# An attention and MLP kernel whose first block runs all scores first, with weights' sums of squares two to four tiles ahead

## Chip, cores and metric

The kernel runs on one core of a Trainium2 chip. The metric is the device time of one execution in microseconds (us), the median over runs.

## The reference

The program is a causal attention with decay, followed by two feed-forward layers. Batch 4, 8 heads, 576 positions, head size 64, model width 512. The part that this document is about is the attention and the first layer:

```python
scores = scale * np.matmul(q, k.transpose(0, 1, 3, 2))
decay = cum[:, :, :, None] - cum[:, :, None, :]        # cum = cumsum(log f)
scores = np.where(causal, -1000000000.0, scores + decay)
attn = np.exp(scores - np.max(scores, axis=-1, keepdims=True))
attn = attn / (np.sum(attn, axis=-1, keepdims=True) + 1e-09)
attn_out = np.matmul(attn, v)
...
xn = (x - mu) / np.sqrt(var + 1e-06) * g_ln            # mu, var over the 512 columns of x
x = x + np.maximum(xn @ w_ch1, 0.0) @ w_ch2            # w_ch1 512x2048, w_ch2 2048x512
...
return (gated @ w_out)                                 # second layer, untouched by the change
```

The weights arrive as 64-bit floats, so the kernel reads each as two 32-bit words.

## The kernel before, in words

The 4 x 576 rows are cut into eight blocks of 256 rows (`BLOCKS`) and a rest, and each block goes through attention, a normalisation and the first layer. Blocks 0 and 1 hold the first 128 positions of two batch entries each; their attention is `attention32`, in f32. It takes the heads in four pairs `p` (p0 to p3), and a pair has four 128x128 squares (two batch entries, two heads):

- scores (L356): the contraction has 66 rows, 64 of the head and two that bring the decay. VectorE (DVE) adds the mask and takes the minimum (L359), ScalarE (ACT) takes the exponential and its sum (L361), then the sums get their 1e-9 (L364) and DVE their reciprocal (L365).
- transposes (L373): a matmul of `e` with `diag`, a diagonal of the reciprocals that DVE writes (L369), which transposes and normalises in one. ACT copies the result out as `PT` (L374).
- P.V (L381): `PT` times the values `vr`, per batch entry once with 128 columns of `vr` and once with the first 64 overwriting the upper half; ACT copies it out as `xT` (L382).

Before these come the loads and the decay rows (`decays`, L146): ScalarE takes the logarithm of `f`, VectorE scans it, and a small tile `decay` goes by two DMAs into the last two rows of `qk` (L343). `WARM` = 54 matmuls of a tile of ones run on TensorE in the meantime (L1064).

The first layer of block 0 (group 0 of `mlp`, L654) is in f32: for each of 16 weight tiles, `ph` (L708) is the product with `w_ch1`, ACT's relu gives `hh` (L715), and `acc` (L693) adds the product with `w_ch2`, two tiles later (`AHEAD`). In the same stretch the kernel narrows every raw weight tile from 64 to 32 bits (`narrow`, L518: two ACT instructions L531 and L532 that write `wt` and `low`, three DVE instructions L533 to L535), adds up the squares of the weights on TensorE (`squares`, L561, into `gram`), and takes from them a scale (`scales`, L575). With the scale it splits each tile into two f16 halves (`make16`, L593: ACT L598, DVE L601) that groups 1 to 7 multiply with. Three raw tiles fit (`RAWB`), and a raw tile's load can start when the third one before it has been narrowed.

The order on each engine comes from a scheduler, which takes the instructions in the order of `events` (L1119 to L1145) and from ordering edges (`after`, L123). `PACE` and `LOWAT` place the ACT work of the first tiles behind marks; `SUMS` says which `ph` waits for the scale; `WSC`, `MAKE` and `VN` are the due times of `scales`, `make16` and `vnorm` (L228, the sums of squares of the values).

Of the kernel before, what the change touches and what calls it, by code (L numbers as in the profile page):

```python
# [30 lines left out]
BUFS0 = dict(vr=1, qk=1, e=3, diag=2, PT=2, st=4)  # L31
# [8 lines left out]
WARM = 54  # L40
# [46 lines left out]
class Kernel:  # L87
# [58 lines left out]
    def decays(self, wk):  # L146


        nc = self.nc
        n = B * H  # L150

        ft = wk.tile([n, S], F32, name="ft")
        for c, queue in ((0, nc.sync), (2 * H, nc.scalar)):
            queue.dma_start(out=ft[c : c + 2 * H], in_=self.f[c : c + 2 * H].rearrange("(n h) s -> h n s", n=2))
        nc.scalar.preload_act_table_set("natural_log_exp_and_others")
        decay = self.decay = self.at.tile([n, 2, 2 * P], F32, name="decay")
        dec1 = wk.tile([n, 2, 3 * P], F32, name="dec1")
# [3 lines left out]
        for t, r, w in ((decay, 1, P), (dec1, 1, P), (f32(dec), 2, S)):  # L161
            nc.gpsimd.memset(t[:, :r, w:], 1.0)
            nc.gpsimd.memset(t[:, r:, :w], 1.0)
        lg = wk.tile([n, S], F32, name="lg")
        cum = wk.tile([n, S], F32, name="cum")

        for cs in (slice(0, P), slice(P, S)):
            nc.vector.tensor_scalar(out=ft[:, cs], in0=ft[:, cs], scalar1=1e-4, scalar2=1.0, op0=ALU.max, op1=ALU.min)
            nc.scalar.activation(lg[:, cs], ft[:, cs], AF.Ln)
            if cs.start:  # L170
                nc.vector.tensor_tensor(out=lg[:, P : P + 1], in0=lg[:, P : P + 1], in1=cum[:, P - 1 : P], op=ALU.add)
            nc.vector.tensor_tensor_scan(out=cum[:, cs], data0=one[:, cs], data1=lg[:, cs], initial=0.0, op0=ALU.mult, op1=ALU.add)
# [8 lines left out]
        nc.scalar.activation(dec[:, 2, S:], f32(h), AF.Copy, scale=-1.0)  # L181
        nc.scalar.activation(dec[:, 3, S:], f32(l), AF.Copy, scale=-1.0)
        nc.scalar.dma_start(out=self.gT, in_=self.moe_g_ln)
        self.gscale(wk)
# [3 lines left out]
    def gscale(self, wk):  # L188

        nc = self.nc  # L190
        g = wk.tile([P, DM], F32, name="gall")
# [3 lines left out]
        nc.scalar.dma_start(out=g, in_=self.moe_g_ln.rearrange("p k -> (p k)").partition_broadcast(P))  # L195
        nc.vector.tensor_reduce(out=m, in_=g, axis=mybir.AxisListType.X, op=ALU.max, apply_absolute_value=True)
# [126 lines left out]

    def attention32(self, b, xT):
# [9 lines left out]
        tags = ("s2", "s2", "av") if b else ("acc", "ph", "av")  # L334
        qka = at.tile([66, NP, 2, 2, 2 * P], F32, tag="qk", name="qk", bufs=bufs["qk"])
# [14 lines left out]
        for p in range(NP):  # L350
            qk, vr = qka[:, p], vra[:, :, p * P : (p + 1) * P]
            ps, e, diag = bank(tags[0]), four("e"), four("diag")
            st = at.tile([P, 2, 4], F32, tag="st", name="st", bufs=bufs["st"])
            four_ = [(n, u, 2 * n + u) for n in range(2) for u in range(2)]
            for n, u, c in four_:
                mm(ps[:, n, u], lhsT=qk[:, u, n, :P], rhs=qk[:, u, n, P:], start=True, stop=True, skip_group_check=True)  # L356
# [9 lines left out]
            yield  # L366

            ps, pt = bank(tags[1]), four("PT")
# [3 lines left out]
            for n, u, c in four_:  # L372
                mm(ps[:, n, u], lhsT=e[:, n, u], rhs=diag[:, n, u], start=True, stop=True, skip_group_check=True)  # L373
# [4 lines left out]
            for n in range(2):  # L378
# [3 lines left out]
            nc.scalar.activation(xT[:, p].rearrange("p (n w) -> p n w", n=2), pav[:, 0], AF.Copy)  # L382
# [135 lines left out]
    def narrow(self, raw, tmp, low=None):  # L518
# [10 lines left out]
        else:  # L529
# [3 lines left out]
            nc.vector.tensor_scalar(out=a, in0=a, scalar1=F64_LO * 2.0**16, scalar2=F64_HI * 2.0**16, op0=ALU.max, op1=ALU.min)  # L533
            nc.vector.scalar_tensor_tensor(out=low, in0=hi, scalar=0x80000000, in1=low, op0=ALU.bitwise_and, op1=ALU.bitwise_or)
            nc.vector.scalar_tensor_tensor(out=b, in0=b, scalar=3, in1=low, op0=ALU.logical_shift_left, op1=ALU.bitwise_or)  # L535
# [3 lines left out]
    def load_raw(self, j):  # L539
# [6 lines left out]
        nc.sync.dma_start(out=raw[:, DM:], in_=self.moe_w_ch2[cs, :])  # L546

    def load_w(self, j):
# [5 lines left out]
        first = self.narrow(raw, w, self.st.tile([P, 2 * DM], U32, tag="low", name="low", bufs=2))  # L554
# [3 lines left out]
        if j < len(LOWAT):  # L558
            self.after(self.low, self.done[LOWAT[j]])

    def squares(self, j):  # L561
# [52 lines left out]
    def norm(self, x, s, y, whole, end, c):  # L614
# [9 lines left out]
        for t in range(NK):  # L624
            nc.vector.tensor_tensor(out=c[:, t, :], in0=x[:, t, :], in1=pm, op=ALU.subtract)
# [28 lines left out]
    def mlp(self, g, states, y):  # L654
# [386 lines left out]
    def run(self):  # L1041
# [20 lines left out]
        warm, ones = self.bank("s2"), self.ones.bitcast(BF16)  # L1062
        for i in range(WARM):
            self.nc.tensor.matmul(warm[:, : 2 * P], lhsT=ones[:, :P], rhs=ones, start=True, stop=True)  # L1064
# [17 lines left out]
        def prep(n):  # L1082
# [25 lines left out]
            g = self.norm(xT, s, y, g > 0, n >= last - 1, xc)  # L1108
            while True:
# [16 lines left out]
        events += [(MAKE + 0.02 * j if j < SOON else G1 + 0.5 * (j - SOON + 0.5) / (NF + 1), -1, NF + 2 + j) for j in range(NF)]  # L1126
        events += [(WSC, -1, NF + 1)] + [(VN + 0.05 * i, -1, NF) for i in range(B + 2)]
        events += [(at, -2, j) for j, at in enumerate(RAWAT)]
# [152 lines left out]
```

## Time and profile before

| | us |
|---|---|
| median of three runs | 790.7 |
| lowest and highest | 788.97, 794.69 |
| the profiled execution | 788.37 |
| its span (first to last instruction) | 786.7 |
| TensorE busy in the span | 763.1 |

The profiled execution lies 2.3 us below the median, and its span covers all but 1.7 us of it. The profile names engines PE (TensorE matmuls), PEld (its weight loads), DVE (VectorE), ACT (ScalarE), POOL (GpSimd) and SP (SyncE, which issues DMAs). L356 is line 356 of the kernel. An f32 matmul is recorded as two matmuls, so "x8" behind one stands for four in the code.

### The profile page before, as it was taken

What the parts mean: (1) busy time and instruction counts of PE and PEld (TensorE: products, weight loads), DVE (VectorE), ACT (ScalarE), POOL (GpSimd) and SP (SyncE); (2) the same over time, 40 slices, a digit from 0 to 9 for tenths busy, and PEclk for the clock granted to TensorE, in tenths of its full rate; (3) what the DMA queues carried; (4) which work ended last, traced back from release to release, by engine and by line L of the source; (5) the groups of instructions that cost most, each with busy time, mean ns of one, the idle gap of its engine ahead of it and who ended that gap; (6) DMA issues with size and microseconds to landing.
All of it is one profiled execution on the core that took longest, in us unless ns stands there. A gap on an engine that the chain in (4) does not pass through costs nothing.

```text
span 786.7 us, 16302 instructions
## 1 busy us (share of the span) xinstructions
PE 763.1 (97%) x5978; PEld 581.1 (74%) x5978; DVE 549.5 (70%) x1490; ACT 521.0 (66%) x1315; POOL 59.8 (8%) x89
## 2 busy tenths in 40 slices
PE   8799999999999999999999999999999999999998
PEld 7588887887877877778888888544447668668676
DVE  5699589849389889979858955688425672654634
ACT  5787489849388889878858854485417643656543
POOL 3100011011011001100201100100021000000000
PEclk8999999999999999999999999999999999999999
DMA  8888576366678998997995964831034320000101
GB/s 252 215 308 307 183 221 93 56 153 119 152 201 160 196 242 151 197 204 156 195 184 117 130 97 145 208 125 54 1 64 73 112 69 1 33 29 9 54 1 61
DMA packets 164227, 104.72 MB, mean 133 GB/s; under 512 B 106178, under 2 KB 151362, under 8 KB 164148
## 3 DMA queue, kind: packets, MB, share of 16 engines
q1 hardware_dynamic: 157848, 96.63, 50.5%
q0 software_dynamic: 5296, 5.28, 5.5%
q10 hardware_dynamic: 1004, 1.78, 0.8%
q8 instruction: 47, 0.77, 0.4%
q14 instruction: 32, 0.26, 0.1%
HBM read 64.37 MB, written 15.11 MB: 101 GB/s over the span
## 4 chain that ended last, share of the span: by engine, by line
PE 69%; DVE 13%; ACT 7%; DMA 6%; issue 3%; SPq 1%; POOL 1%; DVEq 0%; ACTq 0%; POOLq 0%
PE ph L708 16%; PE acc L693 14%; PE pb L649 8%; PE pb L650 8%; PE pb L648 8%; PE s L296 3%; PE av L460 3%; DMA vr<-in_v_dram 2%; DVE P L317 1%; PE s L693 1%; PE av L381 1%; DMA PT<-P 1%; PE gram L569 1%; DVE hl L719 1%; DVE wt L601 1%
## 5 line engine op out<-in xcount | busy, mean ns | idle before, releaser
L693 PE MATMUL acc<-hh,wt 128*128 128x256 f16 (+2 forms) x960 | 196.9, 295 | 1.1 <-DVE t L736 0.5
L708 PE MATMUL ph<-xh,wt 128*128 128x256 f16 (+1 forms) x896 | 187.8, 289 | 5.6 <-DVE hl L719 5.0
L708 PEld LDWEIGHTS <-wt 128*128 128x128 f16 x1344 | 127.3, 98 | 52.0 <-issue 13.6
L693 PEld LDWEIGHTS <-wt 128*128 128x128 f16 x1344 | 128.7, 98 | 43.8 <-issue 5.3
L708 PE MATMUL ph<-xl,wt 128*128 128x256 f16 (+1 forms) x448 | 129.6, 289 | 0.0
L693 PE MATMUL acc<-hl,wt 128*128 128x256 f16 (+1 forms) x416 | 115.3, 281 | 0.0
L715 ACT ACTIVATE hh<-ph 128x256 f16<-128x256 f32 (+2 forms) x128 | 51.0, 399 | 58.5 <-PE ph L708 58.3
L719 DVE SCALAR_TENSOR_TENSOR hl<-ph,hh 128x256 f16<-128x256 f32 (+1 forms) x112 | 50.7, 455 | 39.7 <-ACT hh L715 39.3
L261 ACT ACTIVATE P<-sd,st 128x512 f16<-128x512 f32 (+1 forms) x128 | 70.6, 587 | 10.9 <-DVE st L307 9.5
L317 DVE SCALAR_TENSOR_TENSOR P<-sd,st,P 128x384 f16<-128x384 f32 (+1 forms) x96 | 58.7, 634 | 9.3 <-ACT P L261 8.8
L304 ACT ACTIVATE sd<-sd,st 128x384 f32<-128x384 f32 (+2 forms) x80 | 54.6, 682 | 15.1 <-DVE st L300 14.9
L296 PE MATMUL s<-x 68*128 68x384 f32 (+7 forms) x256 | 63.3, 360 | 0.1
L300 DVE CUSTOM_DVE_ANT_0 sd<-s,mask 128x384 f32<-128x384 f32 (+2 forms) x80 | 45.9, 580 | 4.7 <-PE s L296 3.7
L740 POOL DMA_DIRECT2D x_d<-t x36 | 32.4, 1089 | 185.3 <-DVE t L736 148.9
L261 ACT ACTIVATE x<-qk 64x320 fp32r<-64x320 f32 (+1 forms) x64 | 41.4, 698 | 0.9 <-DMA qk<-in_qk_dram 0.9
L1016 DVE SCALAR_TENSOR_TENSOR u<-pb,wsc,u 128x288 f32<-128x288 f32 x32 | 16.0, 515 | 34.5 <-PE pb L1015 34.5
L296 PEld LDWEIGHTS s<-x 68*128 68x128 f32 (+3 forms) x256 | 36.9, 177 | 2.7 <-issue 1.0
L648 PE MATMUL pb<-x2h,wil 128*128 128x288 f16 (+2 forms) x144 | 37.8, 273 | 0.0
L650 PE MATMUL pb<-x2h,wih 128*128 128x288 f16 (+2 forms) x144 | 37.7, 273 | 0.0
L649 PE MATMUL pb<-x2l,wih 128*128 128x288 f16 (+2 forms) x144 | 37.7, 273 | 0.0
L648 PE MATMUL pb<-wsh,vl 128*128 128x288 f16 x128 | 36.6, 286 | 0.1
L650 PE MATMUL pb<-wsh,vh 128*128 128x288 f16 x128 | 36.6, 286 | 0.0
(281 smaller groups left out, 1597.7 us busy)
## 6 DMA issues: line engine op xcount, KB each, us to landing
raw<-in_moe_w_ch_dram SPq DMA_DIRECT2D x32, 512.0 KB
qk<-in_qk_dram SPq DMA_DIRECT2D x32, 448.0 KB
vraw<-in_v_dram SPq DMA_DIRECT2D x5, 1024.0 KB
vr<-in_v_dram SPq DMA_DIRECT2D x16, 320.0 KB
x_d<-xT SPq DMA_DIRECT2D x9, 512.0 KB
x_d<-t POOLq DMA_DIRECT2D x36, 128.0 KB, 4.4
out_dram<-o SPq DMA_DIRECT2D x32, 144.0 KB
raw<-in_moe_w_in_dram SPq DMA_DIRECT2D x8, 512.0 KB
```

Of the source, the lines that this page charges most:

```text
L261: self.nc.scalar.activation(out, in_, AF.Copy, scale=scale)
L296: nc.tensor.matmul(ps[: R * u + R, : c1 - c0], lhsT=x[:, lo - q0 - R * u : hi - q0], rhs=y[:, c0:c1], start=g == 0, stop=g == len(heads[u] ...
L300: nc.vector.tensor_tensor_reduce(out=sd[:M, c0:c1], in0=ps[:M, : c1 - c0], in1=mask, scale=-0.125, scalar=3e38 if n == 0 else st[:M, n - 1 ...
L304: nc.scalar.activation(sd[:M, :N], sd[:M, :N], AF.Exp, bias=st[:M, n : n + 1], scale=-1.0, accum_out=st[:M, 2:3])
L317: low = nc.vector.scalar_tensor_tensor(out=dl, in0=src, scalar=rs, in1=dh, op0=ALU.mult, op1=ALU.subtract)
L648: first = mm(out, lhsT=al, rhs=bh, start=start, stop=False, **kw)
L649: mm(out, lhsT=ah, rhs=bl, start=False, stop=False, **kw)
L650: mm(out, lhsT=ah, rhs=bh, start=False, stop=stop, **kw)
L693: ins = nc.tensor.matmul(acc[m], lhsT=a, rhs=b, start=bank not in clear, stop=last and e == len(terms) - 1, skip_group_check=True)
L708: ins = nc.tensor.matmul(ph, lhsT=a, rhs=b, start=k == e == 0, stop=k == NK - 1 and e == len(terms) - 1)
L715: relu = nc.scalar.activation(hh, ph, AF.Relu)
L719: nc.vector.scalar_tensor_tensor(out=hl, in0=ph, scalar=0.0, in1=hh, op0=ALU.max, op1=ALU.subtract)
```

## The change

The core of the diff (lines left out are "..."):

```diff
-BUFS0 = dict(vr=1, qk=1, e=3, diag=2, PT=2, st=4)
+BUFS0 = dict(vr=1, qk=1, e=4, diag=2, PT=2, st=4)
...
-WARM = 54
+WARM, FILLS = 52, (4, 12, 6)
...
-PACE = (1, "split", "split", "split", "split")
-LOWAT = (1, 2, 3)
-SUMS = 13
+PACE = (1, "x3", "split", "split", "split")
+LOWAT = (1, "x3", "split")
+SUMS = 14
+REST = 0.1
+SQ = (1, 3, 4, 5, 6, 8, 9, 10, 12, 13, 14, 16)
...
-WSC, MAKE, VN = 0.63, 0.64, 0.7
+WSC, MAKE, VN = 0.76, 0.765, 0.82
...
+    def fill(self, n, behind=None):
+        ones = self.ones.bitcast(BF16)
+        for i in range(n):
+            ins = self.nc.tensor.matmul(self.warm[:, : 2 * P], lhsT=ones[:, :P], rhs=ones, start=True, stop=True)
...
@@ attention32
+        if not b:
+            self.vm = at.tile([P, 2, NP, 2, P], F32, name="vm")
+            for u in range(2):
+                clear = nc.vector.memset(self.vm[:, :, :, u, 64 - 64 * u : P - 64 * u], 0.0)
...
-                    loads.append(nc.sync.dma_start(out=row, in_=self.decay[b * H : (b + 2) * H, r]))
-                loads.append(nc.sync.dma_start(out=vra, in_=self.v[b : b + 2, :P].rearrange("b p d -> p b d")))
+                    queue = nc.scalar if r and not b else nc.sync
+                    loads.append(queue.dma_start(out=row, in_=self.decay[b * H : (b + 2) * H, r]))
+        loads.append(nc.sync.dma_start(out=vra, in_=self.v[b : b + 2, :P].rearrange("b p d -> p b d")))
+        for u in range(2):
...
+            nc.gpsimd.tensor_copy(out=vm[:, :, :, u, us], in_=v[:, :, :, us])
...
+        def scores(p):
+            qk = qka[:, p]
+            ps, e = bank("s2" if p > 1 else tags[0]), four("e")
...
+            if not b and p % 2:
+                self.fill(FILLS[p // 2], ins)
...
+        for p in range(NP):
+            for i in range(len(ahead), min(p + 2, NP) if b else NP):
+                ahead.append(scores(i))
+                yield
+            e, st = ahead[p]
...
-                for u in (1, 0):
-                    mm(pav[: 64 * u + 64, 0, n], lhsT=vr[:, n, : 64 * u + 64], rhs=pt[:, n, u], start=True, stop=True, skip_group_check=True)
+            for n, u, c in four_:
+                ins = mm(pav[:, 0, n], lhsT=vm[:, n, p, u], rhs=pt[:, n, u], start=u == 0, stop=u == 1, skip_group_check=True)
+            if not b and p == NP - 1:
+                self.fill(FILLS[2], ins)
...
@@ load_raw
-        nc.sync.dma_start(out=raw[:, DM:], in_=self.moe_w_ch2[cs, :])
+        second = nc.sync.dma_start(out=raw[:, DM:], in_=self.moe_w_ch2[cs, :])
+        if j == 0:
+            self.after(second, self.marks["loads"])
...
@@ mlp, behind the ph matmuls of tile j
+            if g == 0:
+                self.marks["hidden"] = ins
+                for i in range(SQ[j - 1] if j else 0, SQ[j]) if j < len(SQ) else ():
+                    self.squares(i)
...
@@ run, behind load_w(n)
-                    if n >= len(CONV):
-                        for i in range(n + 1) if n == len(CONV) else [n]:
-                            self.squares(i)
```

In words: block 0 computes the scores of all four pairs before the first transpose, with 4 matmuls of ones behind p1 and 12 behind p3; 6 more stand behind the last P.V (`FILLS`). P.V now takes `vm`, the values in two halves beside zeros, so that every product is 128 columns wide and two of them add up in one bank. VectorE clears `vm` and GpSimd fills it. Block 1's scores run a pair ahead of its transposes. The squares of weight tile `i` are emitted behind `ph` of an earlier tile (`SQ`). The raw weights are all loaded after the attention's loads, the second decay row goes by ScalarE's queue, `gscale` moves out of `decays` to behind block 0's normalisation (its load by GpSimd's queue), two `dec` rows are written by GpSimd in place of ScalarE, two memsets move from GpSimd to VectorE, and block 0's square sums for the normalisation are put off to the event `REST`.

The order on ScalarE, at the end of block 0's attention, before (numbers behind a tile's name tell its copies apart; `raw_215` is weight tile 0, `raw_218` tile 1):

```order
L374 ACTIVATE PT_243<-ph_242 128x512
L361 ACTIVATE e_324,st_326<-e_324,st_326 128x128 x4
L374 ACTIVATE PT_275<-ph_274 128x512
L531 ACTIVATE wt_201<-raw_215 128x1024
L532 ACTIVATE low_377<-raw_215 128x1024
L364 ACTIVATE st_326<-st_326 128x4
L382 ACTIVATE xT_205<-av_250 128x256
L374 ACTIVATE PT_309<-ph_308 128x512
L532 ACTIVATE low_397<-raw_218 128x1024
L382 ACTIVATE xT_205<-s2_282 128x256
L382 ACTIVATE xT_205<-av_316 128x256
L374 ACTIVATE PT_342<-ph_341 128x512
```

and the same place now (L387, L390, L408, L416 are the former L361, L364, L374, L382; L566 and L567 the former L531 and L532):

```order
L387 ACTIVATE e_272,st_273<-e_272,st_273 128x128 x3
L390 ACTIVATE st_255<-st_255 128x4
L408 ACTIVATE PT_301<-ph_300 128x512
L390 ACTIVATE st_273<-st_273 128x4
L408 ACTIVATE PT_316<-ph_315 128x512
L567 ACTIVATE low_379<-raw_207 128x1024
L566 ACTIVATE wt_188<-raw_207 128x1024
L416 ACTIVATE xT_192<-av_309 128x256
L408 ACTIVATE PT_333<-ph_332 128x512
L416 ACTIVATE xT_192<-s2_324 128x256
L408 ACTIVATE PT_349<-ph_348 128x512
L416 ACTIVATE xT_192<-av_341 128x256
```

All exponentials of the block now stand ahead of its first `PT`, and one weight tile's words stand between the `PT`s in place of one and a half, with the second one's behind the last `xT`.

The order on TensorE from the first transpose of block 0, before:

```order
L373 MATMUL ph_242<-diag_226,e_225 128x128 x4
L373 MATMUL ph_274<-diag_258,e_257 128x128 x4
L381 MATMUL av_250<-PT_243,vr_207 128x128
L381 MATMUL av_250<-PT_243,vr_207 64x128
```

and now:

```order
L407 MATMUL ph_300<-diag_302,e_217 128x128 x4
L407 MATMUL ph_315<-diag_317,e_234 128x128 x4
L413 MATMUL av_309<-PT_301,vm_193 128x128 x4
L407 MATMUL ph_332<-diag_334,e_255 128x128 x4
L413 MATMUL s2_324<-PT_316,vm_193 128x128 x4
L407 MATMUL ph_348<-diag_350,e_272 128x128 x4
L413 MATMUL av_341<-PT_333,vm_193 128x128 x4
```

The order of pairs is the same; a P.V of a pair is four equal products where it was two wide and two narrow ones in turn.

## Rows read from the trace of the kernel before

**Rows 1.** The page: span, busy time by engine, and PE's clock in 40 slices.

```profile
span 786.7 us, 16302 instructions
PE 763.1 (97%) x5978; PEld 581.1 (74%) x5978; DVE 549.5 (70%) x1490; ACT 521.0 (66%) x1315; POOL 59.8 (8%) x89
PEclk8999999999999999999999999999999999999999
```

**Rows 2.** Stretches: from:to, length, PE busy (instructions), granted clock, DMA share, GB/s.

```profile
9.03:12.44 3.41, 2.44 (x20) 0.99 0.91 279
12.50:22.50 10.00, 9.41 (x39) 0.50 1.08 346
23.00:39.50 16.50, 11.74 (x68) 1.00 0.75 195
45.30:124.60 79.30, 79.30 (x550) 1.00 0.76 236
129.50:132.00 2.50, 1.51 (x6) 0.97 0.63 129
132.00:135.00 3.00, 2.42 (x12) 0.50 0.25 68
```

**Rows 3.** Timeline, 0 to 40 us: start, length, engine, line, operation, idle before.

```profile
0.91 0.17 DVE L135 MEMSET onesf<- 128x128 f32 x1 [0.91 <-PEq L1270]
...
1.27 8.15 PE L1064 MATMUL s<-ones 128*128 128x256 bf16 x54 [1.27 <-DVE eps L140]
...
3.68 1.41 DVE L168 TENSOR_SCALAR ft<-ft 32x128 f32<-32x128 f32 x2 [2.46 <-DMA ft<-in_f_dram]
...
10.04 2.05 PE L356 MATMUL acc<-qk 66*128 66x128 f32 x16 [0.62 <-DMA qk<-decay]
...
11.69 0.40 ACT L361 ACTIVATE e<-e,st 128x128 f32<-128x128 f32 x1 [0.73 <-DVE st L359]
...
12.09 0.39 ACT L361 ACTIVATE e<-e,st 128x128 f32<-128x128 f32 x1
...
21.42 0.58 ACT L374 ACTIVATE PT<-ph 128x512 f32<-128x512 f32 x1
21.89 1.10 ACT L531 ACTIVATE wt<-raw 128x1024 f32<-128x1024 f32 x1
...
30.82 0.39 ACT L382 ACTIVATE xT<-s 128x256 f32<-128x256 f32 x1 [0.70 <-PE s L381]
...
33.77 1.56 PE L708 MATMUL ph<-xg,wt 128*128 128x256 f32 x6 [1.25 <-ACT xg L672]
```

**Rows 4.** Chain that ended last, 40 to 100 us: start, length, what.

```profile
43.59 1.73 PE acc L693 x8
45.31 0.46 PE gram L569 x8
...
83.69 1.42 PE av L381 x8
...
92.52 0.94 PE s L373 x8
```

**Rows 5.** Timeline of DVE: one weight tile's narrowing, and the last tile's end.

```profile
47.52 0.69 DVE L533 TENSOR_SCALAR wt<-wt 128x1024 f32<-128x1024 f32 x1
...
48.13 1.22 DVE L534 SCALAR_TENSOR_TENSOR low<-raw,low 128x1024 uint32<-128x1024 uint32 x1
...
49.26 1.22 DVE L535 SCALAR_TENSOR_TENSOR wt<-wt,low 128x1024 uint32<-128x1024 uint32 x1
...
91.15 1.23 DVE L535 SCALAR_TENSOR_TENSOR wt<-wt,low 128x1024 uint32<-128x1024 uint32 x1
```

**Rows 6.** Timeline of PE and DVE at the passage from group 0 to group 1.

```profile
124.59 0.27 PE L708 MATMUL ph<-xh,wt 128*128 128x256 f16 x1
...
132.58 0.37 PE L708 MATMUL ph<-xh,wt 128*128 128x256 f16 x1 [0.72 <-DVE hl L719]
...
132.84 0.74 DVE L601 SCALAR_TENSOR_TENSOR wt<-wt,w1c 128x512 f16<-128x512 f32 x1
```

More of the change, by code (lines that the diff above doesn't have):

```diff
@@ L160, in decays @@
         nc.gpsimd.memset(one, 1.0)
-        for t, r, w in ((decay, 1, P), (dec1, 1, P), (f32(dec), 2, S)):
-            nc.gpsimd.memset(t[:, :r, w:], 1.0)
-            nc.gpsimd.memset(t[:, r:, :w], 1.0)
+        for e, t, r, w in ((nc.gpsimd, decay, 1, P), (nc.vector, f32(dec), 2, S), (nc.gpsimd, dec1, 1, P)):
+            e.memset(t[:, :r, w:], 1.0)
+            e.memset(t[:, r:, :w], 1.0)
         lg = wk.tile([n, S], F32, name="lg")
@@ L171, in decays @@
                 nc.vector.tensor_tensor(out=lg[:, P : P + 1], in0=lg[:, P : P + 1], in1=cum[:, P - 1 : P], op=ALU.add)
-            nc.vector.tensor_tensor_scan(out=cum[:, cs], data0=one[:, cs], data1=lg[:, cs], initial=0.0, op0=ALU.mult, op1=ALU.add)
+            self.scan = nc.vector.tensor_tensor_scan(out=cum[:, cs], data0=one[:, cs], data1=lg[:, cs], initial=0.0, op0=ALU.mult, op1=ALU.add)
             if cs.start == 0:
@@ L180, in decays, with gscale @@
         nc.vector.scalar_tensor_tensor(out=l, in0=cum, scalar=8.0, in1=f32(h), op0=ALU.mult, op1=ALU.subtract)
-        nc.scalar.activation(dec[:, 2, S:], f32(h), AF.Copy, scale=-1.0)
-        nc.scalar.activation(dec[:, 3, S:], f32(l), AF.Copy, scale=-1.0)
+        for r, x in ((2, h), (3, l)):
+            nc.gpsimd.tensor_scalar(out=dec[:, r, S:], in0=f32(x), scalar1=-1.0, scalar2=1.0, op0=ALU.mult, op1=ALU.mult)
         nc.scalar.dma_start(out=self.gT, in_=self.moe_g_ln)
-        self.gscale(wk)
         nc.gpsimd.dma_start(out=self.decay1_d, in_=dec1)
         nc.gpsimd.dma_start(out=self.decay_d, in_=f32(dec[:, :, 2 * P :]))
-    def gscale(self, wk):
+    def gscale(self):
         nc = self.nc
-        g = wk.tile([P, DM], F32, name="gall")
+        g = self.at.tile([P, DM], F32, name="gall")
         m = self.cst.tile([P, 1], F32, name="gmax")
@@ L321, in weights @@
         return low
+    def fill(self, n, behind=None):
+        ones = self.ones.bitcast(BF16)
+        for i in range(n):
+            ins = self.nc.tensor.matmul(self.warm[:, : 2 * P], lhsT=ones[:, :P], rhs=ones, start=True, stop=True)
+            if behind is not None:
+                self.after(ins, behind)
+                behind = None
     def attention32(self, b, xT):
@@ L349, in attention32 @@
         yield
-        for p in range(NP):
-            qk, vr = qka[:, p], vra[:, :, p * P : (p + 1) * P]
-            ps, e, diag = bank(tags[0]), four("e"), four("diag")
+        def scores(p):
+            qk = qka[:, p]
+            ps, e = bank("s2" if p > 1 else tags[0]), four("e")
             st = at.tile([P, 2, 4], F32, tag="st", name="st", bufs=bufs["st"])
-            four_ = [(n, u, 2 * n + u) for n in range(2) for u in range(2)]
             for n, u, c in four_:
-                mm(ps[:, n, u], lhsT=qk[:, u, n, :P], rhs=qk[:, u, n, P:], start=True, stop=True, skip_group_check=True)
+                ins = mm(ps[:, n, u], lhsT=qk[:, u, n, :P], rhs=qk[:, u, n, P:], start=True, stop=True, skip_group_check=True)
+                if b and p == c == 0:
+                    self.after(ins, self.first)
+            if not b and p % 2:
+                self.fill(FILLS[p // 2], ins)
             for n, u, c in four_:
@@ L365, in attention32 @@
             nc.vector.reciprocal(st[:, 1], st[:, 1])
-            yield
-            ps, pt = bank(tags[1]), four("PT")
+            return e, st
+        four_ = [(n, u, 2 * n + u) for n in range(2) for u in range(2)]
+        ahead = []
+        for p in range(NP):
[3 more added lines that the diff above has]
+            e, st = ahead[p]
+            ps, pt, diag = bank(tags[1]), four("PT"), four("diag")
             nc.vector.tensor_tensor(
@@ L515, in tail, with narrow @@
         return d[:, c : c + n].rearrange("(k p) t -> p k t", p=P)
-    def narrow(self, raw, tmp, low=None):
+    def narrow(self, raw, tmp, low=None, behind=None):
         nc = self.nc
@@ L532, in narrow @@
             self.low = nc.scalar.activation(low.bitcast(I32), lo, AF.Copy, scale=LOW)
-            nc.vector.tensor_scalar(out=a, in0=a, scalar1=F64_LO * 2.0**16, scalar2=F64_HI * 2.0**16, op0=ALU.max, op1=ALU.min)
-            nc.vector.scalar_tensor_tensor(out=low, in0=hi, scalar=0x80000000, in1=low, op0=ALU.bitwise_and, op1=ALU.bitwise_or)
-            nc.vector.scalar_tensor_tensor(out=b, in0=b, scalar=3, in1=low, op0=ALU.logical_shift_left, op1=ALU.bitwise_or)
+            clip = nc.vector.tensor_scalar(out=a, in0=a, scalar1=F64_LO * 2.0**16, scalar2=F64_HI * 2.0**16, op0=ALU.max, op1=ALU.min)
+            sign = nc.vector.scalar_tensor_tensor(out=low, in0=hi, scalar=0x80000000, in1=low, op0=ALU.bitwise_and, op1=ALU.bitwise_or)
+            self.joined = nc.vector.scalar_tensor_tensor(out=b, in0=b, scalar=3, in1=low, op0=ALU.logical_shift_left, op1=ALU.bitwise_or)
+            if behind is not None:
+                self.after(clip, behind)
+                self.after(sign, behind)
         return first
@@ L553, in load_w @@
         raw, w = self.raw.pop(j), self.wt[:, j + 2]
-        first = self.narrow(raw, w, self.st.tile([P, 2 * DM], U32, tag="low", name="low", bufs=2))
+        first = self.narrow(raw, w, self.st.tile([P, 2 * DM], U32, tag="low", name="low", bufs=2), self.marks["centre"] if j == 1 else None)
+        if j == 2:
+            self.marks["third"] = self.joined
         at = PACE[j] if j < len(PACE) else NP + j - len(PACE)
@@ L558, in load_w @@
         if j < len(LOWAT):
-            self.after(self.low, self.done[LOWAT[j]])
+            self.after(self.low, self.marks[LOWAT[j]] if isinstance(LOWAT[j], str) else self.done[LOWAT[j]])
     def squares(self, j):
@@ L569, in squares @@
             ins = mm(self.gram[:, o], lhsT=top[:, c], rhs=top[:, c], start=j == n == 0, stop=j == NF - 1 and n % NK == NK - 1, skip_group_check=True)
+            if n == 0:
+                self.after(ins, self.marks["hidden"])
             if j == n == 0:
@@ L624, in norm @@
         for t in range(NK):
-            nc.vector.tensor_tensor(out=c[:, t, :], in0=x[:, t, :], in1=pm, op=ALU.subtract)
+            centred = nc.vector.tensor_tensor(out=c[:, t, :], in0=x[:, t, :], in1=pm, op=ALU.subtract)
+        self.marks.setdefault("centre", centred)
         yield
@@ L1061, in run @@
         self.at = at_cm.__enter__()
-        warm, ones = self.bank("s2"), self.ones.bitcast(BF16)
-        for i in range(WARM):
-            self.nc.tensor.matmul(warm[:, : 2 * P], lhsT=ones[:, :P], rhs=ones, start=True, stop=True)
+        self.warm = self.bank("s")
+        self.fill(WARM)
         with self.pool("dk") as dk:
@@ L1108, in prep @@
             g = self.norm(xT, s, y, g > 0, n >= last - 1, xc)
+            if n == 0:
+                with self.tc.high_priority(1):
+                    next(g)
+                self.rest = g
+                return xc
             while True:
@@ L1125, in run @@
         events += [(CONV[j] if j < len(CONV) else G1 * (j - len(CONV) + 0.5) / (NF + 1), -1, j) for j in range(NF)]
-        events += [(MAKE + 0.02 * j if j < SOON else G1 + 0.5 * (j - SOON + 0.5) / (NF + 1), -1, NF + 2 + j) for j in range(NF)]
-        events += [(WSC, -1, NF + 1)] + [(VN + 0.05 * i, -1, NF) for i in range(B + 2)]
-        events += [(at, -2, j) for j, at in enumerate(RAWAT)]
+        events += [(MAKE + 0.001 * j if j < SOON else G1 + 0.5 * (j - SOON + 0.5) / (NF + 1), -1, NF + 2 + j) for j in range(NF)]
+        events += [(WSC, -1, NF + 1)] + [(VN + 0.04 * i, -1, NF) for i in range(B + 2)]
+        events += [(at, -2, j) for j, at in enumerate(RAWAT)] + [(REST, -1, -1)]
         events += [(BEGIN[-2] + M2A + (e + 0.5) / M2S, 2, last) for e in range(26)]
```

22 lines of the change are left out of this document (15 added, 7 removed).

## The prediction

> **What bounds the kernel now.** I read the page first. PE is busy for 763.1 of 786.7 us [rows 1], so the kernel is bound by TensorE, and what can be won is the time in which PE waits, runs at the lower clock, or does what it needn't. Next I asked for stretches of the span. From 45.3 to 124.6 us PE is busy for all of the 79.3 us at full clock [rows 2]: whatever brings the kernel to its 45.3 us mark sooner is won in full, as long as the other engines keep up. Before that mark it looks different. From 12.5 to 22.5 us the granted clock is 0.50 (the 1.2 GHz level) with PE nearly always at work, and from 23.0 to 39.5 us PE is idle for 16.5 - 11.74 = 4.8 us [rows 2]. The timeline says why: the exponentials, copies and narrowing of block 0 run one behind another on ACT, the last `xT` ends at 30.82 + 0.39 = 31.2 us, and the first `ph` starts at 33.77 us [rows 3]. The mark itself is the end of the first `acc`, 43.59 + 1.73 = 45.3 us [rows 4]. A second soft place is the passage to group 1: 1.0 us of idle PE in 129.5 to 132, and 132 to 135 at clock 0.50 [rows 2].
>
> **The change part by part**, against the profiled execution's 788.4 us.
>
> *Start.* 52 matmuls of ones in place of 54 end at 1.27 + 52 x 8.15/54 = 9.1 us [rows 3]. The first scores then waited 0.62 us for a decay row and began at 10.04 [rows 3]; the second row now goes by ACT's queue beside the first, and no weights are loaded ahead of it. Between 9.1 and 10.0 I take 9.4. One thing speaks against: two memsets of 1152 elements now stand on DVE ahead of the clip of `f`, which began at 3.68 us. A memset of 128 took 0.17 us [rows 3]; by length two of the new ones take 3.1 us, end at about 4.3 and delay the rows by 0.6 us, inside the bounds. (The Trainium skill, "VectorE: DVE Perf Modes", section "Zero memsets can be issued as uint32 (trn2)", has a memset take one cycle per element, at the 0.96 GHz of that page's table. By that, an estimate, two take 2.4 us and end before 3.68, with nothing delayed. The row for 128 is 0.04 us over the page's 0.13; no row shows 1152.)
>
> *Block 0 on ACT.* The first exponential followed the first score's start by 11.69 - 10.04 = 1.65 us [rows 3], so now it comes at 11.05. Sixteen follow at a pitch of 0.40 [rows 3], 6.4 us; with 0.2 for the short corrections of the sums between them they end at 17.65. The scores of p2 and p3 don't hold them up: PE has two pairs in 2.05 us [rows 3], its 4 fills are 0.6, so it is through with all four pairs by 9.4 + 4.7 = 14.1. Behind that, in the queue's new order, at 0.58 a `PT`, 0.39 an `xT` and 1.10 for each of the two word instructions of a tile [rows 3] (L532 taken as L531): two `PT` to 18.8, tile 0's words to 21.0, `xT`, `PT`, `xT`, `PT` to 22.9. Then the last P.V, 0.94 on PE, and the last `xT` end at 24.3, against 31.2 before. From there to the first `ph` it took 33.77 - 31.21 = 2.6 us; block 1's masked scores no longer stand in the way on DVE, but tile 1's words, 2.2 us, now stand ahead of `xg` on ACT, so I keep 2.6. First `ph` at 26.9: **6.9 us sooner**.
>
> *From the first `ph` to the mark.* Before, 33.77 to 45.3, 11.5 us, with waits for `xg`, the normalisation's sums and tile 1, and a stretch at half clock. Now PE's queue holds `ph`, squares, block 1's scores of two pairs, `ph`, squares, `acc`: 3 x 1.73 + 2 x 0.46 + 2.05 = 8.2 us [rows 3, 4], mark at 35.1. Tile 1's three DVE instructions (0.61 + 1.13 + 1.14 = 2.9 us by their starts [rows 5]) follow the centring, and end at about 30.5, before the second `ph` is due at 31.1. **3.3 us sooner**, with a pair of scores more done.
>
> *The stretch without waits.* Of its 79.3 us the pair of scores is already done (-1.0, half of 2.05). P.V of a pair took 1.42 us where four equal 128-column products, the transposes, took 0.94 [rows 4]. The new P.V has that shape, so I take 0.94; the bounds are 0.94 and 1.42. Four pairs: -1.9. Clearing and filling `vm` is hidden: GpSimd has nothing else to do before PE wants it at about 18.2. Without that cover the first P.V would wait, at most for four copies. Group 1 then starts at 35.1 + 76.4 = 111.5 in place of 124.59 [rows 6]: **13.1 us sooner**.
>
> *What I give back.* (a) The cover of that stretch is the narrowing. DVE needs 2.9 us a tile; 15 tiles are 43 us, with some 7 us for block 1's masks and diagonals it would be done at 26.9 + 50 = 77 us. PE wants the last tile for its squares, 27 us of work before group 1, at 84.4. DVE holds, by 7 us; the raw loads, each behind the third tile before it, may not. If the last tile came no sooner than now, at 91.15 + 1.23 = 92.4 [rows 5], 8.0 us would be lost. Between 0 and 8.0 I take 1.5, nearer to the DVE row, since it shows the work and not today's pacing. (b) Clock: taken as full, with 0.5 for a stretch that falls; between 0 and 3 (below). (c) The passage: VectorE was busy throughout there with halves of weights at 0.74 [rows 6]. The values' norms move out of it (`VN` 0.82), and the five tiles that group 1 begins with are still split before it. Today's loss there is 1.0 idle, 0.6 idle and 2.42/2 = 1.2 by the clock, 2.8 in all [rows 2]; between 0 and 2.8 I take 1.0 as won. (d) A path laid by hand has no hand-overs between engines: an estimate of 25 at 0.06 is 1.5. (e) The scheduler also lays blocks 2 to 5 in another order, with the same instructions: between -3 and +3, taken as 0.
>
> Sum: 13.1 - 1.5 - 0.5 + 1.0 - 1.5 = 10.6 us. 788.4 - 10.6 = 777.8; the median of the runs shown is 2.3 above the profiled execution, so 790.7 - 10.6 = 780.1 us is the forecast. Late next is the last tiles' narrowing and then the scale.
>
> **The rivals.** *The raw weights pace group 0.* For it: three raw tiles, and DVE instructions that today already run to 92.4 us; against: DMA moved 236 GB/s in that stretch and 346 earlier [rows 2], so there is room. It costs 8.0 in place of 1.5: gain 4.1, 786.6 us. *The clock falls all the same.* For it: in 9.03 to 12.44 us PE was idle for only 1.0 us of 3.4, and the next ten ran at half clock [rows 2]; the new order has gaps of about 1 us before the `PT`s of p2 and p3 too. Against: the fills stand in the worst gaps. Half clock from 12.4 to 22.7 doubles two pairs of scores (+2.05), three transposes (+2.8) and two P.V (+1.9), of which ACT's queue hides more than half; 3 us are left: gain 7.6, 783.1 us. *Group 1 starves, and the kernel is slower.* The scale is due later (`WSC` 0.63 to 0.76), and so are all halves. If it weren't ready before group 1's start, sixteen tiles of two halves at 0.74, 23.7 us on a VectorE that is full there, would stand in front of PE: 780.1 + 23.7 = 804 us. It decides from the point where the scale comes less than five tiles' work (7.4 us) before group 1. Against it: in the new order the scale's matmul stands some 22 us of PE work before group 1. *The gain is lost in the middle.* The other order of blocks 2 to 5 costs over 3 us on top; about 785.
>
> **How the numbers follow.** A measurement of this kernel can tell about 1%, 7.9 us, from no change, so the border is 782.8 us. Chances: the forecast 0.62, the raw weights 0.15, the clock 0.13 (a third of it under the border), the middle 0.05, starving 0.05. Faster by over 1%: 0.62 + 0.05 = 0.67. Within 1%: 0.15 + 0.08 + 0.05 = 0.28. Slower: 0.05. The range goes from the forecast with the passage's whole 2.8, no loss to the weights and 2 from the middle (780.1 - 1.8 - 1.5 - 2.0, 775) to the raw weights' time, 787.
>
> **What would show it.** Right: first `ph` near 27 us, first `acc` ended near 35, no clock under 1.0 between 9 and 45, P.V of a pair near 0.94, group 1's first matmul near 111 to 113, PE at full busy share from 35 to there. Wrong: PE waiting for L570 or for raw weights in 40 to 90; a slice of clock 0.50 before 30 us; PE waits for L645 behind group 1's start; or an early start that is gone again by 500 us.

## The result, and the profile after

The changed kernel takes 781.03 us (median of 4 runs, 777.64 to 782.07), the kernel before 790.47 beside it: a ratio of 0.9866, interval 0.9824 to 0.9908, faster by 1.3%, just past the 1% that can be told from no change (the interval reaches a little under it). The forecast was 780.1. Measured once more later, beside its own runs of before, it was 782.44 against 789.64 (0.9895, 0.9872 to 0.9919), so the gain is 7 to 9 us. By ratio the two measurements of this one kernel are 0.3% (some 2 us) apart, and an edit below that moves the time by less than about 3 us isn't told apart from it. The profiled execution took 781.8 us, with a span 6.6 us shorter than before. The page of the changed kernel answers to [rows 1]:

```profile
span 780.1 us, 16355 instructions
...
PE 755.4 (97%) x5998; PEld 579.8 (74%) x5998; DVE 549.5 (70%) x1494; ACT 519.2 (67%) x1313; POOL 61.9 (8%) x94
...
PEclk9999899999999999999999999999999999999999
```

PE is busy for 7.7 us less, and idle for 24.7 us where it was 23.6. Some 3.6 of the 7.7 are half clock that is gone, and 4.1 are work that is no longer done (an estimate from PE's busy time and granted clock in stretches of 2 us). The low slice of the clock at the start is gone, and a new one stands at slice 5, 78 to 97 us. The stretches of the changed kernel (from:to, length, PE busy, clock, DMA share, GB/s), against [rows 2]:

```profile
9.03:12.44 3.41, 3.25 (x29) 1.00 1.04 278
12.50:22.50 10.00, 8.68 (x74) 1.00 1.05 365
23.00:39.50 16.50, 14.10 (x95) 1.00 1.08 304
45.30:86.00 40.70, 40.70 (x290) 1.00 0.87 286
86.00:97.00 11.00, 7.16 (x29) 0.69 0.79 243
...
132.00:135.00 3.00, 3.00 (x33) 1.00 0.08 16
```

The first 86 us run as forecast: no half clock, more work in PE. Then 11 us have 3.84 us of idle PE and a mean clock of 0.69. The timeline of the start, with DVE, PE and ACT, against [rows 3]:

```profile
1.40 1.02 DVE L164 MEMSET dec<- 32x1152 f32 x1 [0.18 <-issue]
...
3.68 0.52 DVE L170 TENSOR_SCALAR ft<-ft 32x128 f32<-32x128 f32 x2
...
9.19 2.02 PE L378 MATMUL acc<-qk 66*128 66x128 f32 x16 [0.65 <-DMA qk<-decay]
...
18.16 1.06 PE L413 MATMUL av<-PT,vm 128*128 128x128 f32 x8
19.05 1.06 PE L407 MATMUL ph<-diag,e 128*128 128x128 f32 x8
...
23.97 0.38 ACT L416 ACTIVATE xT<-s 128x256 f32<-128x256 f32 x1 [0.51 <-PE s L413]
...
26.86 1.99 PE L753 MATMUL ph<-xg,wt 128*128 128x256 f32 x8 [1.29 <-ACT xg L717]
...
33.26 1.94 PE L738 MATMUL acc<-hh,wt 128*128 128x256 f32 x8
```

The last `xT` ends at 24.35 us, the first `ph` starts at 26.86, the mark stands at 35.20; P.V. of a pair takes 0.89 from its start to the next instruction's. Now the new loss, on the timelines of PE, then ACT, then SP's queue:

```profile
84.72 1.94 PE L738 MATMUL acc<-hh,wt 128*128 128x256 f32 x8
86.50 0.62 PE L611 MATMUL gram<-wt 128*128 128x128 bf16 x8
90.96 0.59 PE L220 MATMUL s<-vq,ones 128*128 128x1 f32 x2 [3.84 <-ACT vp L218]
91.40 2.05 PE L442 MATMUL s<-qk 66*128 66x256 f32 x4
93.25 3.43 PE L753 MATMUL ph<-xg,wt 128*128 128x256 f32 x8
96.52 1.89 PE L738 MATMUL acc<-hh,wt 128*128 128x256 f32 x8
...
90.39 0.42 ACT L218 ACTIVATE vp<-vr 128x256 f16<-128x256 f32 x1 [8.89 <-DMA vr<-in_v_dram]
...
75.46 1.88 SPq L240 DMA_DIRECT2D vraw<-in_v_dram  x2
...
80.10 0.39 SPq L437 DMA_DIRECT2D vr<-in_v_dram  x1
```

Behind the squares of the last tile, PE's queue holds L220, the sum of squares of block 2's first values. ACT makes its operand from `vr`, which is issued at 80.10 behind two loads of `vraw` of 1 MB each, and used at 90.39. The next `ph` stands behind L220 in the queue. After the wait the four scores take 2.05 us and the `ph` 3.43, at half clock; at full clock the rows have 1.11 (old_pv, below) and 1.89: 2.5 us more. In the kernel before, the same sum (L218) came without a wait:

```profile
99.59 0.39 SPq L402 DMA_DIRECT2D vr<-in_v_dram  x1
...
103.64 0.42 ACT L216 ACTIVATE vp<-vr 128x256 f16<-128x256 f32 x1 [0.29 <-DMA vr<-in_v_dram]
...
105.43 0.33 PE L218 MATMUL s<-vq,ones 128*128 128x1 f32 x2
```

There it stood in PE's queue behind the `ph` of 14 of group 0's 16 tiles; the new order has it behind those of 12. Marks of both kernels in us (the stores are the issue of a group's first result tile on GpSimd):

| | before | after | sooner |
|---|---|---|---|
| first `ph` | 33.77 | 26.86 | 6.9 |
| end of the first `acc` | 45.32 | 35.20 | 10.1 |
| first `ph` of group 1 | 124.59 | 120.43 | 4.2 |
| group 0's first store | 124.67 | 121.35 | 3.3 |
| group 3's | 322.23 | 315.43 | 6.8 |
| group 6's | 499.81 | 493.13 | 6.7 |
| span | 786.7 | 780.1 | 6.6 |

In this execution two thirds of what was won by 35 us are gone at group 0's end, and half of that comes back later. In the second profile of the same kernel (after_again, below) the first `ph` of group 1 is at 117.11, 7.5 us sooner than before, and the span is 6.0 us shorter: where the gain goes differs between executions.

### The profile page after: what moved, and what is told of

It is laid out like the page before. It is cut to its first block, busy times and chain, and to the rows that moved or that the text cites. A ratio compares the mean times of both kernels' runs of the same rounds, so it can differ in the third digit from the quotient of the medians.

```text
span 780.1 us, 16355 instructions
## 1 busy us (share of the span) xinstructions
PE 755.4 (97%) x5998; PEld 579.8 (74%) x5998; DVE 549.5 (70%) x1494; ACT 519.2 (67%) x1313; POOL 61.9 (8%) x94
## 3 DMA queue, kind: packets, MB, share of 16 engines
q10 hardware_dynamic: 892, 1.53, 0.6%
## 4 chain that ended last, share of the span: by engine, by line
PE 69%; DMA 12%; DVE 10%; ACT 6%; issue 3%; SPq 0%; DVEq 0%; ACTq 0%
PE ph L753 17%; PE acc L738 15%; PE pb L694 8%; PE pb L695 8%; PE pb L693 8%; PE s L298 4%; PE av L495 3%; DMA vr<-in_v_dram 2%; DMA raw<-in_moe_w_ch_dram 2%; DMA qk<-in_qk_dram 2%; PE s L442 2%; PE s L738 1%; DMA raw<-in_moe_w_in_dram 1%; DVE low L569 1%; DVE P L319 1%
## 5 line engine op out<-in xcount | busy, mean ns | idle before, releaser
L753 PE MATMUL ph<-xh,wt 128*128 128x256 f16 (+1 forms) x896 | 185.4, 288 | 2.6 <-DVE hl L768 2.6
L306 ACT ACTIVATE sd<-sd,st 128x384 f32<-128x384 f32 (+2 forms) x80 | 54.6, 683 | 15.7 <-DVE st L302 15.4
```

Source lines behind the costliest of these rows:

```text
L306: nc.scalar.activation(sd[:M, :N], sd[:M, :N], AF.Exp, bias=st[:M, n : n + 1], scale=-1.0, accum_out=st[:M, 2:3])
```

## The experiments

All are edits of the changed kernel; the table at the end of this section has every run's marks.

**vraw_behind: the values' loads behind block 2's.**

```diff
-                nc.sync.dma_start(out=t, in_=self.v[b, :512]...)
+                self.after(nc.sync.dma_start(out=t, in_=self.v[b, :512]...), self.marks["v10"])
```

(`v10` is block 2's third `vr` load.)

> The changed kernel with one edge more: the 1 MB loads of vraw stand on SP's queue behind the third vr of block 2 instead of ahead of its first. Theory: the 3.84 us for which PE waits at 87 to 91 us come from the first vr, which lands 10.3 us after its issue because two vraw loads are ahead of it, and the 3.4 us of the next ph in place of 1.9 come from the clock that this wait costs. Then the wait is under 0.5 us, the clock is full in 85 to 100, group 1's first ph comes at 113 to 116 in place of 120.4, and the time is 775 to 778 us. Rival, the transfers as a whole are late (raw weights pace group 0): some other wait of 3 us or more stands in 75 to 100, group 1 starts at 119 or later, and the time stays at 780 to 782. Rival, won before group 1 and lost behind it, as the values' sums now come later: group 1 starts by 116, but the time is within 1 us of 781.

The wait is gone: `vr` is issued at 79.03 and in use at 81.96, the clock is 1.00 from 80 to 100, and group 0's store comes at 115.89, 5.5 us sooner. Group 1's first `ph` is at 116.65, 0.7 later than the theory's bound. The issue and the use:

```profile
79.03 0.39 SPq L437 DMA_DIRECT2D vr<-in_v_dram  x1
...
81.96 0.42 ACT L218 ACTIVATE vp<-vr 128x256 f16<-128x256 f32 x1
```

ACT doesn't wait here, so `vr` took at most 2.9 us. In the five profiles with both `vraw` loads just ahead of it (after, after_again, old_pv and the two of sq_late) it took 8.6 to 10.3, in sq_late_vraw, with none, at most 3.2. So the cause of the wait is shown. But the time is 779.67: 2.7 of the 5.5 us are left in the span, and by its ratio the run can't be told from the changed kernel. No case holds in full; the third, won before group 1 and lost behind it, is nearest. What the wait is worth at the end isn't shown, as the edge also lays blocks 2 to 7 in another order (end of this section).

**vraw_pool: the same loads on GpSimd's queue** (`nc.sync` to `nc.gpsimd` at L240 and L242).

> The changed kernel with all five vraw loads issued from GpSimd's queue, so that SP's queue holds block 2's qk and vr loads and block 1's store with nothing of vraw ahead of them. Theory, the place behind 2 MB on one queue made the first vr late: it lands within 4 us of its issue in place of 10.3, the 3.84 us wait is gone, and group 1's first ph comes at 114 to 118 as with the loads moved back on SP's queue. Rival, it is the bytes, whatever queue they stand on: vr still lands 6 us or more after its issue, and PE waits for 1.5 us or more in 80 to 95. Time by the theory 777 to 781, by the rival 780 to 783.

Half of each. PE no longer waits, and group 1 starts at 116.49. But the `vr` that was issued at 79.34 is used at 86.77, after 7.4 us, with one `vraw` under way on the other queue:

```profile
79.34 0.39 SPq L437 DMA_DIRECT2D vr<-in_v_dram  x1
...
86.77 0.42 ACT L218 ACTIVATE vp<-vr 128x256 f16<-128x256 f32 x1 [1.17 <-DMA vr<-in_v_dram]
```

So bytes under way ahead of it count on another queue too. At 784.05 us it is slower than either case has it; the loss lies behind group 0 (377.8 us to group 6).

**no_fills: without the constant products in block 0.**

```diff
-WARM, FILLS = 52, (4, 12, 6)
+WARM, FILLS = 52, (0, 0, 0)
```

> The changed kernel with its 22 constant products inside block 0 left out (no result changes; they only keep PE at work). Theory, they hold the clock: a stretch at 0.50 appears between 12 and 35 us as in the kernel before, the first ph comes at 28 to 30 us in place of 26.9, and the time is 783 to 785. Rival, ACT sets the pace there and PE's clock hides behind it: a stretch at 0.50 may appear, but the first ph stays within 0.7 us of 26.9 and the time within 1 us of 781. Rival, the clock stays full without them: no stretch under 0.9 before 35 us, and the time is 781.

The stretches of that kernel:

```profile
14.00:16.00 2.00, 0.32 (x3) 1.00 0.99 405
16.00:18.00 2.00, 0.81 (x8) 0.78 1.08 403
18.00:20.00 2.00, 1.99 (x9) 0.50 1.07 376
20.00:22.00 2.00, 2.00 (x12) 0.50 1.05 339
...
32.00:34.00 2.00, 2.00 (x10) 0.50 0.69 241
```

The clock falls to the 1.2 GHz level twice, behind gaps that the fills shorten: before the first transposes PE stood for 2.25 us, in the changed kernel for 0.93. The first `ph` comes at 30.36 (3.5 later), the mark at 40.29 (5.1 later), and the time is 786.74. The theory holds, with `ph` and time a little past its bounds.

**pairwise: block 0's scores in the old order.**

```diff
-            for i in range(len(ahead), min(p + 2, NP) if b else NP):
+            for i in range(len(ahead), min(p + 2, NP) if b else p + 1):
```

> The changed kernel with block 0's scores in the old order: pairs 0 and 1, their transposes and P.V, then pairs 2 and 3 (the fills stay where they are in the code). Theory, the order of block 0 carries the early start: ACT stands behind two round trips through PE again, the last xT ends at 27 to 29 us in place of 24.35, the first ph comes at 29.5 to 31.5 in place of 26.9, and the time is 783 to 786. Rival, ACT's sum of work sets it in either order: the first ph stays within 0.8 us of 26.9, and the time is 780 to 782.

The first `ph` is at 33.93, where the kernel before has it (33.77), and the time is above the theory's bounds too. Without the order of block 0 nothing of the 6.9 us is left. It isn't ACT's queue alone: PE waits 3.59 us before its first transposes, and the clock is at half behind that, which costs another 2.2 us (an estimate from the granted clock in 14 to 20):

```profile
15.20 3.75 PE L407 MATMUL ph<-diag,e 128*128 128x128 f32 x16 [3.59 <-DVE diag L403]
```

So the order and the fills work together, and what each brings doesn't add up (no_fills alone lost 3.5 of the 6.9). The mark, 42.29, is 7.1 late, group 0's store 3.7 late, the end 12.4: the rest is lost behind group 0, first in a wait of 3.2 us for `PT` and half clock behind it at the passage:

```profile
130.00:132.00 2.00, 0.05 (x1) 1.00 1.12 140
132.00:134.00 2.00, 0.74 (x12) 0.56 0.32 40
134.00:136.00 2.00, 2.00 (x14) 0.50 0.03 8
136.00:138.00 2.00, 2.00 (x11) 0.50 0.68 131
```

**old_pv: the old P.V., without `vm`.**

```diff
-            for n, u, c in four_:
-                ins = mm(pav[:, 0, n], lhsT=vm[:, n, p, u], rhs=pt[:, n, u], start=u == 0, stop=u == 1, ...)
+            for n, u in ((0, 1), (0, 0), (1, 1), (1, 0)):
+                ins = mm(pav[: 64 * u + 64, 0, n], lhsT=vra[:, n, p * P : p * P + 64 * u + 64], rhs=pt[:, n, u], start=True, stop=True, ...)
```

> The changed kernel with the old P.V of blocks 0 and 1: products with 64 or 128 columns of the plain vr, the second overwriting, and no vm (no clearing, no GpSimd copies). Theory, the form costs PE time: a pair takes 1.4 us where it takes 0.89 now, 8 pairs make 4 us, of which block 0's four are partly behind ACT: time 783.5 to 785.5. Rival, PE's clearing stands on other waits and nothing is lost: 780 to 782.

```profile
29.47 1.99 PE L753 MATMUL ph<-xg,wt 128*128 128x256 f32 x8 [1.29 <-ACT xg L717]
...
90.77 0.42 ACT L218 ACTIVATE vp<-vr 128x256 f16<-128x256 f32 x1 [6.24 <-DMA vr<-in_v_dram]
...
91.33 0.38 PE L220 MATMUL s<-vq,ones 128*128 128x1 f32 x2 [1.17 <-ACT vp L218]
91.57 1.11 PE L442 MATMUL s<-qk 66*128 66x256 f32 x4
```

The form does cost PE time: the first `ph` and the mark come 2.6 us later. But `vr` is used at 90.77, 0.4 us later than in the changed kernel; PE comes later and waits 2.7 us less (1.17 for 3.84), the clock stays full, and group 0's store is 2.3 us sooner than with the faster form. Against the second profile of the changed kernel, with `vr` in use at 88.03, it is 1.1 us later. The time is 781.24, the rival's: no difference from the faster form can be told. That what PE gains ahead of such a wait is lost in it fits the first pair of profiles; the second doesn't show it.

**b1_pair: block 1's scores without the pair ahead** (`min(p + 2, NP) if b` to `p + 1 if b`).

> The changed kernel with block 1's scores in the old order, each pair's just ahead of its own transposes (block 0 as changed). Theory, group 0's own products fill the time that block 1's exponentials need, and the pair ahead buys little: the mark (end of the first acc) comes up to 1 us sooner as one pair of scores fewer stands ahead of it, group 0 ends within 1.5 us of 121.35, and the time is 779 to 783. Rival, PE stands at block 1's transposes waiting for exponentials or diagonals, 0.5 us or more a pair: 2 us or more of such waits in 35 to 85, and 783 to 786.

Neither. The mark is 0.2 later, since the second `ph` now waits 0.7 us for its weights; PE's waits in 35 to 85 are 1.8 us. Block 2's loads come later with the end of block 1, and nothing holds PE at 87 us: L220 stands behind the `ph` of 15 tiles here, at 100.16, and group 0's store is at 114.46, the soonest of all. The time is 784.94 all the same, since the stretch to group 6 is the longest of all, 382.1 us. A part of that is the mark: group 1's first `ph` comes 2.0 us behind the store here, and 0.9 ahead of it in the changed kernel.

**sq_late: the squares one tile ahead.**

```diff
-SQ = (1, 3, 4, 5, 6, 8, 9, 10, 12, 13, 14, 16)
+SQ = (1, 2, 3, 4, 5, 6, 7, 8, 9, 10, 12, 14, 16)
```

> The changed kernel with the sums of squares one tile a hidden tile at first, so that they run 1 tile ahead and not 2 to 4, and end one hidden tile later. Theory, the place of the squares doesn't bind as long as the scale comes well ahead of group 1: PE's waits in 35 to 85 stay under 2 us, group 1 doesn't wait for halves of weights for more than 1 us, and the time is 779 to 783. Rival, every tile of delay of the scale delays the halves of weights: PE waits for l of the weights behind group 1's start, 3 us or more, and the time is 784 to 788.

774.87 us, under both. No row of PE's waits names halves of weights, and there is no wait at L220, which stands behind the `ph` of 13 tiles: the squares needn't run further ahead. Three kernels then ran side by side: the changed one again, this one again, and this one with the edit of vraw_behind.

> The changed kernel once more, unchanged, beside the two below. Theory, the wait for block 2's vr is part of the program's order and not of one execution: PE waits at L220 for 3 to 4.5 us and ends it at 90 to 91.5 us, group 0's first result store is issued at 120.5 to 122, and the median is 779 to 783. Rival, it was an accident of one execution: the wait is under 2 us.

> The kernel with the squares one tile ahead, once more. Theory, its 6 us over the changed kernel repeat: 773 to 777, 4 to 8 us under the changed kernel beside it, of which 4.3 come before group 0's results (117.0 against 121.35, since PE still has squares to do while the vr is under way) and the rest between groups 1 and 6. Rival, the earlier difference was scatter between runs: within 2 us of the changed kernel.

> The kernel with the squares one tile ahead, and also with the vraw loads behind the third vr of block 2. Theory, each part before group 0's end adds up, and what follows is drawn anew by the order of blocks 2 to 5: group 0's first store at 114 to 117, the stretch from there to group 6's first store between 370 and 380 us as in the runs so far, the rest 287 us, the time 771 to 784 with nothing in the first part to say where. Rival, the part behind group 0 depends on group 0's end alone: it stays within 1 us of the 370.7 of the kernel without the edge, and the time is 771 to 774.

The theory of after_again falls by its numbers: the wait at L220 is there again, but 1.54 us long.

```profile
88.59 0.38 PE L220 MATMUL s<-vq,ones 128*128 128x1 f32 x2 [1.54 <-ACT vp L218]
...
90.00:92.00 2.00, 2.00 (x6) 0.50 1.02 379
```

`vr` is issued 1.2 us sooner than in the first profile and used 2.4 us sooner (88.03), so its landing differs by over 2 us between executions of one program. Group 0's store comes 3.3 us sooner than in the first profile, and the span is 0.6 longer: this execution waits later, 1.94 us for `PT` at 276.6, with the clock at 0.74 around it.

sq_late repeats in its time, 775.38 against 782.44, but not for the reason given: group 0's store is the same as the changed kernel's beside it (117.98, 118.02). Between group 1's and group 3's stores it is 2.8 and 2.9 us shorter in the two pairs of profiles (125.0 for 127.8, 127.4 for 130.3). The changed kernel stands there at the last of block 3's scores, for 2.03 and 2.73 us for `qk`, at a lower clock behind it; sq_late stands there for 1.54 and 0.73 us, and the clock stays full. First the changed kernel again, then sq_late again:

```profile
170.00:180.00 10.00, 7.20 (x52) 0.92 0.80 129
180.00:190.00 10.00, 9.66 (x101) 0.91 0.67 101
```

```profile
170.00:180.00 10.00, 9.27 (x90) 1.00 0.77 132
180.00:190.00 10.00, 9.56 (x100) 1.00 0.81 110
```

sq_late_vraw is as its theory has it, which left a wide range: group 0's store at 115.42, 2.6 us sooner, and the stretch to group 6 back at 374.7: 779.18. All runs (marks from the profiled execution; medians of several):

| run | first `ph` | wait at L220 | group 0's store | from there to group 6's | rest | median | ratio (interval) |
|---|---|---|---|---|---|---|---|
| before | 33.77 | | 124.67 | 375.1 | 286.9 | 790.47 | |
| after | 26.86 | 3.84 | 121.35 | 371.8 | 287.0 | 781.03 | 0.9866 (0.9824 to 0.9908) |
| after_again | 26.82 | 1.54 | 118.02 | 374.3 | 288.3 | 782.44 | 0.9895 (0.9872 to 0.9919) |
| vraw_behind | 26.89 | none | 115.89 | 374.9 | 286.6 | 779.67 | 0.9874 (0.9845 to 0.9902) |
| vraw_pool | 26.86 | none | 115.66 | 377.8 | 286.8 | 784.05 | 0.9941 (0.9914 to 0.9969) |
| no_fills | 30.36 | none | 123.01 | 374.0 | 286.1 | 786.74 | 0.9960 (0.9935 to 0.9986) |
| pairwise | 33.93 | 1.04 | 125.01 | 380.1 | 287.4 | 792.32 | 1.0037 (1.0015 to 1.0059) |
| old_pv | 29.47 | 1.17 | 119.08 | 370.8 | 287.7 | 781.24 | 0.9900 (0.9868 to 0.9932) |
| b1_pair | 27.10 | none | 114.46 | 382.1 | 286.7 | 784.94 | 0.9944 (0.9929 to 0.9958) |
| sq_late | 27.42 | none | 117.01 | 370.7 | 286.9 | 774.87 | 0.9823 (0.9789 to 0.9856) |
| sq_late_again | 26.98 | 1.17 | 117.98 | 371.0 | 286.5 | 775.38 | 0.9817 (0.9792 to 0.9842) |
| sq_late_vraw | 26.90 | none | 115.42 | 374.7 | 286.9 | 779.18 | 0.9870 (0.9845 to 0.9894) |

The rest stays within 2.2 us. The stretch between groups 0 and 6 goes from 370.7 to 382.1, though no edit changes what blocks 2 to 7 compute. The traces have PE, ACT and SP take that stretch in the same sequence (by line and tile) in after, after_again and old_pv, which have 370.8 to 374.3 us, and in the two of sq_late, 370.7 and 371.0. vraw_behind, no_fills and sq_late_vraw share over 90% of ACT's and SP's sequence, and have 374.0 to 374.9. So up to 3.5 us is spread of one order, and the rest goes with the order that the scheduler lays. What differs is PE's idle time, 8.3 to 15.4 us, and what half clock costs, 0 to 4.6; without both, each run has 360 to 364 us left (an estimate from stretches of 2 us). sq_late beats both kernels.

## Why the prediction was right, and where it wasn't

- *Start, ACT's queue, first `ph`, mark*: right. 9.19 for 9.4; last `xT` 24.35 for 24.3; first `ph` 26.86 for 26.9; mark 35.20 for 35.1. pairwise shows that without the order of block 0 the early `ph` is gone, no_fills and old_pv that it needs the fills and the new P.V. as well. The ones ended at 8.53, not 9.1; the wait of 0.65 us for the decay row set the start. The memsets' delay of 0.6 us was not there: two of 1.02 us fill time in which DVE waited for `f`, and the clip starts at 3.68 as before. (The Trainium skill, "VectorE: DVE Perf Modes", section "Zero memsets can be issued as uint32 (trn2)", led to 1.2 us each, an estimate, and to no delay: the trace agrees on the delay; a row is 1.02 us long, 0.2 less, while from the first memset's start to the second's it is 1.21.)
- *P.V. at 0.94*: measured 0.89, against 1.46 in old_pv. But its gain was counted in full in a stretch "without waits", and the time of old_pv shows none lost without it.
- *(a) Weights, 1.5*: no row of PE's waits names L570 in the changed kernel; the last tile's narrowing ends at 83.5 in place of the 77 worked out, and costs nothing. The rival of raw weights falls.
- *(b) Clock, 0.5*: full until 89 us. no_fills shows that the fills keep it so, and that the rival's mechanism was real; its 3 us were 3.5 at the first `ph` and 5.1 at the mark.
- *"13.1 us sooner" at group 1*: this is the step that failed. 4.2 were measured (7.5 in after_again); of the 8.9 missing, 2.0 had been given back under (a) and (b). It took PE's full busy share in 45.3 to 124.6 as a property of the kernel, and asked of the narrowing alone whether it would keep up. It left out block 2's first loads and the sum that needs them. The new order has that sum two tiles sooner in PE's queue, and `vr` behind 2 MB of `vraw`; PE comes to it at 87 us and `vr` is in use at 90.4. The wait is 3.84 us, half clock another 2.5, waits for the normalisation's sums and for `hh` at 36 and 43.7 us another 1.6, and 0.9 are work that now stands ahead of group 1, more of block 2's scores among it.
- *(c) Passage, 1.0 won*: the half clock of 132 to 135 is gone (3.00 busy at 1.00, for 2.42 at 0.50); a wait of 1.62 us for `PT` at 127.6 is new, and so is a lower clock at 180 to 190 (0.83 with PE busy for 9.86), which costs about as much as the half clock that is gone.
- *Group 1 starving*: no row of PE's waits names L645; those for `hl` between 120 and 300 us are 1.5 us, against 4.1 before.
- *(d) Hand-overs, 1.5*: the first `ph` and the mark came within 0.1 us of forecasts that had no hand-overs in them, so none of it shows up to there; behind it no run parts it from other waits.
- *(e) Middle, 0*: from group 0's store to group 6's the changed kernel is 3.4 us shorter, the passage included, in one profile and 0.8 in the other. The band of 3 was a little too narrow for that; the runs, with other orders, span 11.4.

So the sum, 10.6 for 6.6 in the profile and 9.4 and 7.2 in the medians, is near in part by luck: in the first profile two terms missed in opposite directions, 6.9 us too much before group 1, and 2.9 too little behind it (6.6 - 4.2 = 2.4 gained there, where +1.0 - 1.5 had been put). In after_again the first miss is 3.6 (7.5 for 11.1), and 1.5 us are lost behind group 1's start, 1.0 more than put. That group 1 comes later than forecast, 117 to 120 us for 111.5, is in both. Why one order of blocks 2 to 7 is better than another stays open: only that it shows as PE's short waits, those for `qk` and `PT` among the longest, and as the clock behind them.

## What to carry to other kernels

A stretch in which PE never waits is no promise for a kernel that reaches it sooner: look for the transfers that end in it, and ask of each what stands ahead of it and where PE's queue first needs it. A sum in PE's queue that depends on a late load holds up everything ready behind it; issue the small load ahead of the big ones (here that took the wait away, though the time can't be told from the one with it). And where a scheduler lays the program anew, measure several orders: here that was worth nearly as much as the change.

## What the runs showed that was not expected

- The granted clock fell to the 1.2 GHz level behind a wait of 1.54 us at 88.6 (after_again), and not behind 1.17 us at the same instruction (old_pv, 1.00 from 90 to 98) or 1.62 us at 127.6 (after). The clock's part can be as large as the wait: by the granted clock in 88 to 94, an estimate, 1.6 us behind the 1.54; in the first profile of the changed kernel it was 2.5 behind 3.84.
- Moved to another queue, `vraw` still made `vr` late: 7.4 us from issue to use, against at most 2.9 with `vraw` issued behind it.
- The row of a memset of 1152 elements on DVE is 1.02 us long, that of 128 elements 0.17 [rows 3], so rows scaled by length (1.53) give too much. From the start of one memset to the start of the next of the same length it is 1.21 us for 1152 (1.40 to 2.61, after) and 0.14 for 128 (0.91 to 1.05), nearly in proportion.
